# Gated attention and channel mixer on one core: the first turn's scores made in the strip schedule, its operands fetched and rounded on other engines, and the score banks paired by when they come free

## The chip, the core and the metric

The kernel runs on one core of a Trainium2 chip. The metric is the device time of one execution in microseconds (us). Three runs of the kernel before took 1034.19 to 1035.68 us, with a median of 1035.26 us.

## What is computed

Two branches work on the same 2048 tokens of 448 numbers, and a gate mixes them for each token:

```python
g = sigmoid((x * gate_w).sum(-1))
qkv = x @ wqkv                                  # 16 heads of 28
p = softmax(q @ k.T * 28 ** -0.5)               # per head, 2048 x 2048
a = (p @ v) @ wo
b = gelu(layernorm(x) @ w1 + b1) @ w2 + b2      # 448 -> 1792 -> 448
out = g * a + (1 - g) * b
```

## The kernel before

**Strips.** The first part of the program makes q, k and v, then the mixer branch. Every product there is cut into four strips of 32 rows of the TensorE array (partitions 0 to 31, 32 to 63 and so on), which run at the same time. Numbers are held as a rounded high part and the rest as a low part, so a product takes three passes: high by high, high by low, low by high. A planner in the kernel (`Strips.run`) walks through the four strips with a clock of its own, costs and due times, and writes out the order of the instructions once: for each free strip it takes a piece that is under way or opens the next tile in one of the six PSUM banks 0 to 5 (`pick`), and it calls DMAs and roundings when their due time has come (`run_tasks`). The mixer's second product (`Down`, line 503 as all strip work) is evicted by ScalarE (line 410) and stored to `gbs` by a DMA on ScalarE's queue (line 413).

**Row maxima.** Between these pieces stand single matmuls of queries by keys (`RowMax.one`, line 212), each followed by a maximum on VectorE (line 214). They give the shift of the softmax, 1024 of them in all. Some 570 are done within the strips, the rest later.

**Turns.** Attention is a loop of turns, written out by `turn_of` and `batch`. A unit is one head by one block of 128 keys by 512 queries; a turn scores four units (line 1168) and multiplies the four of the turn before by v (line 1212, `batch`). The scores of a unit are three matmuls into one PSUM bank (`score`), each on one strip. A turn has two banks called `first`, two called `second` and two called `spare`; these come from `pairs`, which is turned by one place from turn to turn, so that the six banks 0 to 5 go round in three turns. The order within a turn is: a row maximum into bank 6; the two `first` units alone (step 0); both pairs (steps 1 and 2); then `soften` of the first pair, one exponential on ScalarE over both banks (line 1174); the last pass of the second pair (step 3); `soften` of the second pair, one exponential per bank as long as row maxima are left; a row maximum into the first spare bank; and the products by v in bank 7. `pairs` before holds the first banks 0, 2 and 4, so that a pair is always two neighbouring banks, and the exponential of a pair reads 1024 consecutive words per partition.

**Between strips and turns** stand four matmuls of `idle` (line 974) that compute nothing that is used, and six more after the first turn's scores. The first turn is scored like every other; its keys and queries come by GpSimd's queue (lines 848 and 865), and GpSimd rounds them (lines 853, 854, 869, 870) when the last `Up` piece is done (`early`). Twelve tiles of the output are projected (`project`) in turns near the end, four in the last lines.

Of the kernel before, what the change touches and what calls it, by code (L numbers as in the profile page):

```python
# [7 lines left out]
F32 = mybir.dt.float32  # L8
# [27 lines left out]
def kernel(ctx: ExitStack, tc: tile.TileContext, xt, wqk, wv, wo, xk, w1, b1, w2, b2,  # L36
# [336 lines left out]
    class Down(Piece):  # L373
# [31 lines left out]
        def close(self, st, now):  # L405
            if self.i > 1:
                gb = mhp[0].tile([P, CH], F32, name="h", bufs=2)[:, :D]
            else:
                gb = mhp[0].tile([P, D], F32, name="gb", bufs=2)
            nc.scalar.activation(gb, bk[:, self.bank, :D], AF.Copy)  # L410
            st.use("act", now + 0.2, 0.56)
            st.free[self.bank] = st.act + 0.1
            nc.scalar.dma_start(gbs[self.c * TPC + self.i], gb)
            st.use("act", now, 0.5)

    class Strips:


        def __init__(self, tiles):
            self.tiles = tiles  # L420
            self.t = [0.0] * 4
            self.visit, self.held = [None] * 4, [None] * 4
            self.feed, self.stat = Feed(self, []), Feed(self, bxr)
            self.live = []
            self.free = {b: 0.0 for b in range(6)}
            self.rm = {6: 0.0, 7: 0.0}
            self.dve = self.act = self.pool = -1.0
            self.clock = self.dma = -1.0
# [6 lines left out]
            self.handed = 0  # L435

        def use(self, engine, start, cost):
            setattr(self, engine, max(getattr(self, engine), start) + cost)
# [20 lines left out]
                    self.use(engine, t, cost)  # L459

        def pick(self, s, now, over=None):
            for x in self.live:
                if x.bar(self):
                    continue
                if x.next(s) and not x.busy and x.ready <= now and (over is None or isinstance(x, Up) and x.c == over.c):
                    return x
            if over is None and self.tiles and self.tiles[0].next(s) and self.tiles[0].start(self, now):
                b = min(self.free, key=lambda b: self.free[b], default=None)
                if b is not None and self.free[b] <= now:
                    x = self.tiles.pop(0)  # L470
                    x.bank = b
                    x.begin(s)
                    del self.free[b]
                    self.live.append(x)
                    started(self, x, now)
                    return x
            return None

        def run(self):
            while self.tiles or self.live:  # L480
# [22 lines left out]
                mm = nc.tensor.matmul(bk[:, x.bank, :n], a, b, start=x.first, stop=(len(x.rem) == 1 and m == len(ops) - 1),  # L503
                                      skip_group_check=True)
# [377 lines left out]
    def early(st, now):  # L882

        m0.close()
        st.at(now + 2.0, lambda: nc.scalar.activation(gate, zall, AF.Exp, scale=-1.0), act=1.6)
        st.at(now + 6.0, gates, dve=0.7)
        ak = ctx.enter_context(tc.tile_pool(name="ak", bufs=1, side="right", reuse_waits="tile"))
        ka, kb, la, lb = (ak.tile([P, S], F32R, name=n) for n in ("ka", "kb", "la", "lb"))
        va, vb = (ak.tile([P, NT, P], F32, name=n) for n in ("va", "vb"))
        for d, a, b in ((khi, ka, kb), (klo, la, lb), (vg, va, vb)):  # L890
            d.update({0: a, 1: b, 2: a, 3: b})
        st.at(now + 4.0, lambda: nc.gpsimd.memset(la.bitcast(F32), 0.0), pool=2.2)
# [5 lines left out]
        st.at(now + 10.0, lambda: load_v(0, slice(0, 8)))  # L898
        st.at(now + 11.5, lambda: load_v(0, slice(8, 16)))
        st.at(now + 16.0, lambda: load_ms(0))  # L900
        st.at(now + 23.0, lambda: key_row(0))
        st.at(now + 23.5, lambda: nc.gpsimd.memset(lb.bitcast(F32), 0.0), pool=2.2)

    for v in vt:
        nc.gpsimd.memset(v[:, :, DH:DH + 1], 1.0)
# [61 lines left out]
    m1.close()  # L967
    loads[0] = nc.sync

    pairs = sorted((0, 2, 4), key=lambda b: max(strips.free[b], strips.free[b + 1]))  # L970

    def idle(n, b):
        for _ in range(n):
            nc.tensor.matmul(bk[:, b], khi[0][:, 0:P], khi[0][:, 0:CH], start=True, stop=True)  # L974

    idle(4, min(range(6), key=lambda b: strips.free[b]))

    def sb(name, bufs):
        return ctx.enter_context(tc.tile_pool(name=name, bufs=bufs, reuse_waits="tile"))
# [159 lines left out]
                tail.append((turn + (12 if c == 1 else 8) + i, c * TPC + i))  # L1139

    UNITS = NG * NC * 64
    prob, tail = {}, []
    begins = set()
    projected = set()
    cold = [1] * 4
# [24 lines left out]
    def soften(u, half, b, count, step=4):  # L1170
        t = ap.tile([P, 2, CH], F32, name=f"p{half}")
        for i in range(0, count, step):
            e = min(i + step, count)
            nc.scalar.activation(t[:, i:e], bk[:, b + i:b + e], AF.Exp, scale=SCALE)  # L1174
        for i in range(count):
            prob[u + i] = t[:, i]

    def turn_of(u, turn):

        left = UNITS - u  # L1180
        size = min(left, 4)
        for x in range(u, u + size):
            n = x // 64
            if n not in begins:
                begins.add(n)
                begun(n, turn)
# [3 lines left out]
        ahead = [(u + i) % 4 for i in range(2)]  # L1190
        behind = [(u + i) % 4 for i in range(2, 4)]
        if rowmax.left() and turn not in projected:
            lone(behind, 6, turn)
        for step in range(4):
            for i in range(na):
                if step < 3:
                    score(u + i, step, first + i)
            for i in range(nb):
                if step > 0:
                    score(u + 2 + i, step - 1, second + i)  # L1200
            if step == 2:
                soften(u, 0, first, na)
        if nb:
            soften(u + 2, 1, second, nb, 1 if rowmax.left() else 2)
        if rowmax.left():
            lone(ahead, spare, turn)
        return size

    def batch(b, turn):
# [83 lines left out]
```

## Time and profile before

| | |
|---|---|
| median of three runs | 1035.26 us |
| the profiled execution's own time | 1034.85 us |
| its span, from the first to the last instruction | 1033.1 us |
| TensorE busy | 1024.8 us (99%) |
| VectorE busy | 749.2 us (73%) |
| ScalarE busy | 662.9 us (64%) |
| GpSimd busy | 372.9 us (36%) |
| mean granted TensorE clock | 0.998 |

One execution was taken by the hardware profiler. PE is TensorE's matmuls, PEld its weight loads, ACT is ScalarE, DVE VectorE, POOL GpSimd and SP the engine that issues most DMAs; a q behind a name is that engine's DMA queue. Times count from the first instruction. A timeline row has the start, the length, the engine and the line, the operation with its tiles, and how many instructions were merged into it; in brackets stands how long the engine had stood idle and which engine released it. A group's row has the time that its instructions took together and the mean of one in ns. A row of a table by stretch has the stretch, its length and then the busy time of PE, PEld, DVE, ACT and POOL with the number of instructions, the granted clock, the DMA engines' share and their rate.

### The profile page before, as it was taken

How to read it: one execution, taken by the hardware profiler on the slowest of the kernel's cores; microseconds unless marked ns; L12 is line 12 of the kernel's file. 1: busy time of each engine (PE TensorE's matmuls, PEld its weight loads, DVE VectorE, ACT ScalarE, POOL GpSimd, SP SyncE). 2: the span in 40 equal slices, each digit the busy share in tenths (PEclk: the TensorE clock that was granted, in tenths of full speed). 3: DMA queues.
4: the chain of work that ended last, by engine and by line, in shares of the span. 5: the costliest groups of instructions: out<-in, count | busy, mean ns of one | idle time of the engine just before them, and what ended most of it. 6: DMA issues, size and time to landing. Idle time of an engine off the chain costs nothing.

```text
span 1033.1 us, 30973 instructions
## 1 busy us (share of the span) xinstructions
PE 1024.8 (99%) x13170; PEld 676.9 (66%) x13170; DVE 749.2 (73%) x1178; ACT 662.9 (64%) x1018; POOL 372.9 (36%) x396
## 2 busy tenths in 40 slices
PE   9999999999999999999999999999999999999997
PEld 6999999999999999944444444444444444454555
DVE  4899999999999999956666666656666666644101
ACT  5234365034043043089999999999999999959553
POOL 5467569626334036460011001410111223626414
PEclk9999999999999999999999999999999999999999
DMA  7697533221110013251000010310002201121202
GB/s 242 201 264 250 181 109 101 83 65 45 39 38 11 9 42 87 67 145 29 14 18 26 21 36 15 102 34 24 17 27 59 56 12 58 21 73 31 73 29 81
DMA packets 47787, 73.20 MB, mean 71 GB/s; under 512 B 13840, under 2 KB 28816, under 8 KB 46848
## 3 DMA queue, kind: packets, MB, share of 16 engines
q1 hardware_dynamic: 33888, 39.11, 13.5%
q0 software_dynamic: 5120, 16.89, 5.7%
q10 hardware_dynamic: 8640, 15.21, 4.1%
q8 instruction: 103, 1.69, 0.7%
q14 instruction: 36, 0.29, 0.1%
HBM read 51.75 MB, written 19.31 MB: 69 GB/s over the span
## 4 chain that ended last, share of the span: by engine, by line
PE 98%; DMA 1%; DVE 0%; ACT 0%; SPq 0%; issue 0%; ACTq 0%; DVEq 0%
PE bk L503 36%; PE bk L1212 25%; PE bk L1168 17%; PE bk L212 16%; PE bk L1030 2%; PE bk L1032 1%; PE bk L1031 1%; PE bk L949 1%; DMA first<-in_xt 1%; DVE raw L715 0%; PE bk L974 0%; DVE mx L214 0%; ACT gb L410 0%; PE bk L1095 0%; SPq L927 0%
## 5 line engine op out<-in xcount | busy, mean ns | idle before, releaser
L214 DVE TENSOR_REDUCE mx<-bk 128x1 f32<-128x512 f32 x1024 | 683.7, 689 | 179.6 <-PE bk L212 155.0
L1174 ACT ACTIVATE p<-bk 128x1024 f32<-128x1024 f32 x745 | 510.9, 758 | 63.7 <-PE bk L1168 37.7
L212 PE MATMUL bk<-kd,qd 28*128 28x512 f32 x1024 | 436.1, 427 | 0.7 <-DVE mx L214 0.6
L212 PEld LDWEIGHTS bk<-kd,qd 28*128 28x128 f32 x1024 | 186.1, 182 | 199.5 <-DVE mx L214 176.7
L503 PE MATMUL bk<-yh,w1f 32*128 32x512 f32 x1568 | 186.4, 391 | 0.0
L503 PE MATMUL bk<-yl,w1f 32*128 32x512 f32 x784 | 161.8, 390 | 0.0
L503 PEld LDWEIGHTS bk<-yh,w1f 32*128 32x128 f32 x1568 | 151.1, 183 | 0.7 <-ACT gb L410 0.2
L503 PE MATMUL bk<-w2h,hh 32*128 32x448 f32 x896 | 143.7, 365 | 0.0
L503 PE MATMUL bk<-w2l,hh 32*128 32x448 f32 x896 | 142.5, 363 | 0.0
L1070 POOL TENSOR_TENSOR ot<-ob,rc 128x512 f32<-128x512 f32 x12 | 15.4, 1286 | 348.0 <-DMA rc<-rls 289.4
L1212 PE MATMUL bk<-p,vb 128*32 128x512 f32 x1024 | 136.6, 605 | 0.0
L1212 PE MATMUL bk<-p,va 128*32 128x512 f32 x1024 | 136.4, 605 | 0.0
L367 POOL TENSOR_TENSOR hl<-h,hh 128x512 fp32r<-128x512 f32 x56 | 72.6, 1308 | 124.4 <-PE bk L503 48.3
L503 PEld LDWEIGHTS bk<-yl,w1f 32*128 32x128 f32 x784 | 104.0, 183 | 0.0
L503 PEld LDWEIGHTS bk<-w2h,hh 32*128 32x128 f32 x896 | 103.4, 183 | 0.3
L503 PEld LDWEIGHTS bk<-w2l,hh 32*128 32x128 f32 x896 | 102.9, 183 | 0.1
L1168 PE MATMUL bk<-yh,ka 29*128 29x512 f32 x512 | 93.2, 470 | 0.1
L503 PE MATMUL bk<-w2h,hl 32*128 32x448 f32 x896 | 88.8, 362 | 0.0
L1168 PE MATMUL bk<-yh,kb 29*128 29x512 f32 x512 | 88.1, 477 | 0.0
L359 ACT ACTIVATE h<-bk,b1s 128x512 f32<-128x512 f32 x56 | 38.3, 683 | 67.9 <-PE bk L503 56.9
L1168 PE MATMUL bk<-yh,la 28*128 28x512 f32 x512 | 80.3, 393 | 0.0
L1168 PE MATMUL bk<-yl,ka 28*128 28x512 f32 x512 | 79.7, 390 | 0.0
(141 smaller groups left out, 1554.1 us busy)
## 6 DMA issues: line engine op xcount, KB each, us to landing
qk<-qo ACTq DMA_DIRECT2D x28, 256.0 KB
raw<-in_xt SPq DMA_DIRECT2D x17, 256.0 KB
vs<-vt ACTq DMA_DIRECT2D x16, 256.0 KB
rc<-rls SPq DMA_DIRECT2D x60, 64.0 KB
bxr<-in_xk POOLq DMA_DIRECT2D x8, 448.0 KB, 6.0
acc<-gbs SPq DMA_DIRECT2D x16, 224.0 KB
out_y<-acc SPq DMA_DIRECT2D x16, 224.0 KB
qd<-qk SPq DMA_DIRECT2D x60, 56.0 KB
```

The lines of the kernel that those rows point to most:

```text
L212: nc.tensor.matmul(ps, self.qd[n % 2][r, i * P:(i + 1) * P], self.kd[r, k * 512:(k + 1) * 512], start=True, stop=True)
L214: nc.vector.reduce_max(self.mx[n % 2][:, j, i, k:k + 1], ps, axis=AX)
L359: nc.scalar.activation(h, bk[:, self.bank], AF.Gelu_apprx_tanh, bias=b1s[:, f:f + 1])
L367: nc.gpsimd.tensor_sub(hl[f], h, hh[f].bitcast(F32))
L503: mm = nc.tensor.matmul(bk[:, x.bank, :n], a, b, start=x.first, stop=(len(x.rem) == 1 and m == len(ops) - 1), skip_group_check=True)
L949: nc.tensor.matmul(bk[:, b], w, v, start=(i == 0), stop=(i == len(ops) - 1), skip_group_check=True)
L1030: nc.tensor.matmul(po, h, woh[:, g], start=(g == 0), stop=False, skip_group_check=True)
L1031: nc.tensor.matmul(po, h, wol[:, g], start=False, stop=False, skip_group_check=True)
L1070: nc.gpsimd.tensor_mul(ot[g][:, c * CH:(c + 1) * CH], ob, rc)
L1168: nc.tensor.matmul(bk[:, b], w[r, ks], q[r], start=(p == 0), stop=(p == 2), skip_group_check=True)
L1174: nc.scalar.activation(t[:, i:e], bk[:, b + i:b + e], AF.Exp, scale=SCALE)
L1212: nc.tensor.matmul(bk[32 * j:32 * j + 32, 7], vg[n // NC][:, k, 32 * j:32 * j + 32], prob[4 * b + j], start=(k == 0), stop=(k == NT - 1), ...
```

## The change

It has seven parts. A new piece `Unit` scores one of the first four units within the strip schedule: three matmuls on one strip, an exponential into the space of `vg[1]`, open to the planner once no tile is left to open and 16 us of the planner's clock have gone by since the last `Up` piece. The loop of turns then starts at unit 4, so that turn 0 scores units 4 to 7 and multiplies units 0 to 3 by v. The keys and queries of the first units are fetched by SyncE with earlier due times, the high parts are made by ScalarE, the low parts by GpSimd, and the row of ones goes into the unrounded keys. The last four mixer tiles are stored by SyncE. The ten `idle` matmuls are gone. `pairs` is no longer (0,1), (2,3), (4,5): the six banks are sorted by the time at which the planner has them free, and taken two by two, so a pair can be two banks that are not neighbours; `soften` reads them with a step between the banks. In turns after a projection the two halves of the units may change places.

```diff
+    SCORED = 16.0
...
             nc.scalar.activation(gb, bk[:, self.bank, :D], AF.Copy)
...
+            if self.c == NC - 1:
+                nc.sync.dma_start(gbs[self.c * TPC + self.i], gb)
+                return
             nc.scalar.dma_start(gbs[self.c * TPC + self.i], gb)
...
+    class Unit(Piece):
+        cost = 0.235
...
+        def start(self, st, now):
+            return st.scored <= now
+
+        def ops(self, s):
+            r, top = slice(32 * s, 32 * s + DH), slice(32 * s, 32 * s + DH + 1)
+            h, l, q, ql_ = khi[0], klo[0], qh[0], ql[0]
+            return [(h[top, 0:P], q[top]), (l[r, 0:P], q[r]), (h[r, 0:P], ql_[r])]
+
+        def close(self, st, now):
+            t = vg[1][:, 4 * self.i:4 * self.i + 4].rearrange("p t d -> p (t d)")
+            nc.scalar.activation(t, bk[:, self.bank], AF.Exp, scale=SCALE)
+            prob[self.i] = t
...
         def pick(self, s, now, over=None):
+            if over is None and not self.tiles:
+                x = next((x for x in self.units if x.next(s) and x.start(self, now)), None)
...
-        st.at(now + 4.0, lambda: nc.gpsimd.memset(la.bitcast(F32), 0.0), pool=2.2)
+        loads[0] = nc.sync
+        st.scored = now + SCORED
+        st.at(now + 0.3, lambda: nc.gpsimd.memset(la.bitcast(F32), 0.0), pool=1.9)
         for j in range(4):
-            st.at(now + 3.5 + 1.5 * j, lambda j=j: fetch_qq(0, j))
-            st.at(now + 6.5 + 1.5 * j, lambda j=j: fetch_kk(0, j))
-            st.at(now + 14.5 + 2.0 * j, lambda j=j: split_kk(0, j), pool=1.9)
-        st.at(now + 12.0, lambda: split_qq(0), pool=1.9)
...
+            st.at(now + 0.6 + 0.6 * j, lambda j=j: fetch_qq(0, j))
+            st.at(now + 3.5 + 0.6 * j, lambda j=j: fetch_kk(0, j))
+        st.at(now + 3.2, lambda: loads[0].dma_start(la[DH:P:32].bitcast(F32), ones))
+
+        def high(h, l):
+            nc.scalar.activation(h, l.bitcast(F32), AF.Copy)
...
+                nc.gpsimd.tensor_sub(l, l.bitcast(F32), h.bitcast(F32))
...
-    pairs = sorted((0, 2, 4), key=lambda b: max(strips.free[b], strips.free[b + 1]))
-
-    def idle(n, b):
-        for _ in range(n):
-            nc.tensor.matmul(bk[:, b], khi[0][:, 0:P], khi[0][:, 0:CH], start=True, stop=True)
-
-    idle(4, min(range(6), key=lambda b: strips.free[b]))
+    order = sorted(range(6), key=lambda b: strips.free[b])
+    pairs = [sorted(order[i:i + 2]) for i in (0, 2, 4)]
...
-            nc.scalar.activation(t[:, i:e], bk[:, b + i:b + e], AF.Exp, scale=SCALE)
+            nc.scalar.activation(t[:, i:e], bk[:, b[i]:b[e - 1] + 1:b[1] - b[0]], AF.Exp, scale=SCALE)
...
+        if turn in projected and size == 4 and sum(rowmax.cnt[s] for s in behind) < sum(rowmax.cnt[s] for s in ahead):
+            ahead, behind, order = behind, ahead, [2, 3, 0, 1]
...
-    u = b = turn = 0
+    u, b, turn = 4, 0, 0
+    begins.add(0)
+    begun(0, 0)
...
-        if turn == 0:
-            idle(6, 7)
```

**From the strips to the turns, on TensorE.** The program before has, behind the last strip matmul (`w2h`, `hl`), the dummies, the twelve score matmuls of turn 0 (keys `ka` and `la`, queries `yh` and `yl`), more dummies and the first row maximum (`kd`, `qd`) of turn 1:

```order
L503 MATMUL bk<-w2h_3803,hl_2961 128x448 x2
L974 MATMUL bk<-ka 128x512 x4
L1168 MATMUL bk<-yh,ka 128x512 x2
L1168 MATMUL bk<-yh,la 128x512 x2
L1168 MATMUL bk<-yh,ka 128x512 x2
L1168 MATMUL bk<-yl,ka 128x512 x2
L1168 MATMUL bk<-yh,la 128x512 x2
L1168 MATMUL bk<-yl,ka 128x512 x2
L974 MATMUL bk<-ka 128x512 x6
L212 MATMUL bk<-kd,qd_153 128x512
```

The changed program, at the same place; `vb` holds the exponentials of units 0 to 3:

```order
L543 MATMUL bk<-w2h_3803,hl_2961 128x448
L1218 MATMUL bk<-yh,ka 128x512 x2
L1218 MATMUL bk<-yh,la 128x512 x2
L1218 MATMUL bk<-yh,ka 128x512 x2
L1218 MATMUL bk<-yl,ka 128x512 x2
L1218 MATMUL bk<-yh,la 128x512 x2
L1218 MATMUL bk<-yl,ka 128x512 x2
L1264 MATMUL bk<-vb,va 32x512 x4
L212 MATMUL bk<-kd,qd_153 128x512
```

The dummies are gone, turn 0 has products by v, and the twelve score matmuls of units 0 to 3 have moved up among the strip matmuls, in two groups of six, the first with 142 rows of strip work behind it, the second with 188. One row maximum more stands in the strips (570 for 569), and there are 255 turns with scores instead of 256.

**Within a turn, on TensorE, with the counters that a row waits for.** `Activation_49` counts ScalarE's instructions, `DVE_49` VectorE's. This is turn 2 of the program before, from the `first` scores to the products by v:

```order
L1168 MATMUL bk<-yh,ka 128x512 [waits DVE_49]
L1168 MATMUL bk<-yh,ka 128x512
L1168 MATMUL bk<-yh,la 128x512 x2
L1168 MATMUL bk<-yh,ka 128x512 [waits Activation_49]
L1168 MATMUL bk<-yh,ka 128x512
L1168 MATMUL bk<-yl,ka 128x512 x2
L1168 MATMUL bk<-yh,la 128x512 x2
L1168 MATMUL bk<-yl,ka 128x512 x2
L212 MATMUL bk<-kd,qd_152 128x512 [waits Activation_49]
L1212 MATMUL bk<-p_9804,va 32x512 x2
L1212 MATMUL bk<-p_9808,va 32x512
L1212 MATMUL bk<-p_9808,va 32x512 [waits Activation_49]
```

Its three waits for ScalarE are for exponentials of the turn before, by the counts that the program holds. In the changed program these rows reach from the last score row of turn 3 to the last but one of turn 4:

```order
L1218 MATMUL bk<-yl,ka 128x512 [waits Activation_49]
L212 MATMUL bk<-kd,qd_153 128x512
L1264 MATMUL bk<-p_9845,va 32x512 x2
L1264 MATMUL bk<-p_9849,va 32x512 x2
L212 MATMUL bk<-kd,qd_153 128x512 [waits DVE_49]
L1218 MATMUL bk<-yh,ka 128x512 [waits DVE_49]
L1218 MATMUL bk<-yh,ka 128x512
L1218 MATMUL bk<-yh,la 128x512 x2
L1218 MATMUL bk<-yh,ka 128x512 x2
L1218 MATMUL bk<-yl,ka 128x512 x2
L1218 MATMUL bk<-yh,la 128x512 x2
L1218 MATMUL bk<-yl,ka 128x512 [waits Activation_49]
```

The last pass of the `second` pair (`yl`, `ka` at the end of a turn) now waits for ScalarE, in turn 3 its second matmul, in turn 4 its first, and the count is that of the first exponential of the same turn. In turn 5 it is the row maximum behind the scores that does so:

```order
L1218 MATMUL bk<-yh,la 128x512 x2
L1218 MATMUL bk<-yh,ka 128x512 x2
L1218 MATMUL bk<-yl,ka 128x512 x2
L1218 MATMUL bk<-yh,la 128x512 x2
L1218 MATMUL bk<-yl,ka 128x512 x2
L212 MATMUL bk<-kd,qd_153 128x512 [waits Activation_49]
```

The pairs that the planner's times give are the banks 2 and 5, 1 and 3, 0 and 4. In turns whose number divides by three the exponential of the first pair reads banks 2 and 5, and the row that waits for it writes bank 3; in the next turn it reads 0 and 4, and bank 2 waits; in the third it reads 1 and 3, and the row maximum into bank 2 waits. Of the 255 turns with scores 247 have such a wait for the first exponential of their own turn; the other 8 are turns of the third kind after the last row maximum. In those last turns the exponential of the second pair is one instruction over two banks as well, and the next turn's first matmul into a bank between them waits for it.

More of the change, by code (lines that the diff above doesn't have):

```diff
@@ L435, in __init__ @@
             self.handed = 0
+            self.units, self.scored = [Unit(j) for j in range(4)], 1e9
         def use(self, engine, start, cost):
@@ L461, in pick @@
         def pick(self, s, now, over=None):
+            if over is None and not self.tiles:
+                x = next((x for x in self.units if x.next(s) and x.start(self, now)), None)
+                b = min(self.free, key=lambda b: self.free[b], default=None)
+                if x is not None and b is not None and self.free[b] <= now:
+                    self.units.remove(x)
+                    x.bank = b
+                    del self.free[b]
+                    self.live.append(x)
+                    return x
             for x in self.live:
@@ L479, in run @@
         def run(self):
-            while self.tiles or self.live:
+            while self.tiles or self.live or self.units:
                 s = min(range(4), key=lambda s: (self.t[s], s))
@@ L891, in early, with low @@
             d.update({0: a, 1: b, 2: a, 3: b})
-        st.at(now + 4.0, lambda: nc.gpsimd.memset(la.bitcast(F32), 0.0), pool=2.2)
+        loads[0] = nc.sync
+        st.scored = now + SCORED
+        st.at(now + 0.3, lambda: nc.gpsimd.memset(la.bitcast(F32), 0.0), pool=1.9)
         for j in range(4):
-            st.at(now + 3.5 + 1.5 * j, lambda j=j: fetch_qq(0, j))
-            st.at(now + 6.5 + 1.5 * j, lambda j=j: fetch_kk(0, j))
-            st.at(now + 14.5 + 2.0 * j, lambda j=j: split_kk(0, j), pool=1.9)
-        st.at(now + 12.0, lambda: split_qq(0), pool=1.9)
[L898 to L902, printed above, removed]
+            st.at(now + 0.6 + 0.6 * j, lambda j=j: fetch_qq(0, j))
[3 more added lines that the diff above has]
+            nc.scalar.activation(h, l.bitcast(F32), AF.Copy)
+            st.use("act", st.clock, 0.65)
+            def low():
+                nc.gpsimd.tensor_sub(l, l.bitcast(F32), h.bitcast(F32))
+                st.use("pool", st.clock, 1.35)
+            st.at(st.act + 0.1, low)
+        st.at(now + 7.0, lambda: high(qh[0], ql[0]))
+        for i in range(4):
+            sl = slice(i * CH, (i + 1) * CH)
+            st.at(now + 10.5 + 1.4 * i, lambda sl=sl: high(ka[:, sl], la[:, sl]))
+        st.at(now + 10.6, lambda: load_ms(0))
+        st.at(now + 11.5, lambda: load_v(0, slice(0, 8)))
+        st.at(now + 13.0, lambda: load_v(0, slice(8, 16)))
+        st.at(now + 19.0, lambda: nc.gpsimd.memset(lb.bitcast(F32), 0.0), pool=2.2)
     for v in vt:
@@ L1141 @@
     UNITS = NG * NC * 64
-    prob, tail = {}, []
+    tail = []
     begins = set()
@@ L1189, in turn_of @@
         nb = size - na
-        ahead = [(u + i) % 4 for i in range(2)]
-        behind = [(u + i) % 4 for i in range(2, 4)]
+        ahead, behind = ([(u + i) % 4 for i in x] for x in ((0, 1), (2, 3)))
+        order = list(range(size))
+        if turn in projected and size == 4 and sum(rowmax.cnt[s] for s in behind) < sum(rowmax.cnt[s] for s in ahead):
+            ahead, behind, order = behind, ahead, [2, 3, 0, 1]
         if rowmax.left() and turn not in projected:
@@ L1196, in turn_of @@
                 if step < 3:
-                    score(u + i, step, first + i)
+                    score(u + order[i], step, first[i])
             for i in range(nb):
                 if step > 0:
-                    score(u + 2 + i, step - 1, second + i)
+                    score(u + order[2 + i], step - 1, second[i])
             if step == 2:
-                soften(u, 0, first, na)
+                soften(u + order[0], 0, first, na)
         if nb:
-            soften(u + 2, 1, second, nb, 1 if rowmax.left() else 2)
+            soften(u + order[2], 1, second, nb, 1 if rowmax.left() else 2)
         if rowmax.left():
-            lone(ahead, spare, turn)
+            lone(ahead, spare[0], turn)
         return size
```

6 lines of the change are left out of this document (added).

## Prediction

> **What bounds the kernel now.** First the page's busy times and its chain of waits.
>
> ```profile
> PE 1024.8 (99%) x13170; PEld 676.9 (66%) x13170; DVE 749.2 (73%) x1178; ACT 662.9 (64%) x1018; POOL 372.9 (36%) x396
> ...
> PE bk L503 36%; PE bk L1212 25%; PE bk L1168 17%; PE bk L212 16%; PE bk L1030 2%; PE bk L1032 1%; PE bk L1031 1%; PE bk L949 1%; DMA first<-in_xt 1%; DVE raw L715 0%; PE bk L974 0%; DVE mx L214 0%; ACT gb L410 0%; PE bk L1095 0%; SPq L927 0%
> ```
>
> TensorE is busy 99% of the span, and 98% of the chain is its rows: any time in which it has to stand still is added to the end, and what other engines do in that time is not. So I read next the timeline of TensorE over one turn, the loop that runs 255 times, and ScalarE's row in the same turn.
>
> ```profile
> 446.88 0.50 PE L212 MATMUL bk<-kd,qd 28*128 28x512 f32 x1
> 446.88 0.73 PE L1168 MATMUL bk<-yh,ka 29*128 29x512 f32 x4
> 447.22 0.41 PE L1168 MATMUL bk<-yh,la 28*128 28x512 f32 x3
> 447.46 0.39 PE L1168 MATMUL bk<-yl,ka 28*128 28x512 f32 x2
> ...
> 447.69 0.38 PE L212 MATMUL bk<-kd,qd 28*128 28x512 f32 x1
> 448.01 1.07 PE L1212 MATMUL bk<-p,va 128*32 128x512 f32 x8
> 449.01 0.49 PE L212 MATMUL bk<-kd,qd 28*128 28x512 f32 x1
> ```
>
> ```profile
> 447.96 1.02 ACT L1174 ACTIVATE p<-bk 128x1024 f32<-128x1024 f32 x1 [0.19 <-PE bk L1168]
> ```
>
> The turn starts at 446.88 and the next at 449.01: 2.13 us. The first pair's last pass (`yl`, `ka`) starts at 447.46 and ends at 447.85; the exponential of that pair runs from 447.96 to 448.98. The second pair's last pass and the row maximum beside it start at 447.69, the products by v at 448.01. What matters: in this kernel the second pair's last pass is long over when the first pair's exponential ends. Over 500 us the lengths are the same every time:
>
> ```profile
> L1174 ACT ACTIVATE p<-bk 128x512 f32<-128x512 f32 x459 | 248.7, 600 | 0.0
> L1174 ACT ACTIVATE p<-bk 128x1024 f32<-128x1024 f32 x230 | 235.4, 1023 | 40.6 <-PE bk L1168 15.2 <-PE bk L212 0.8
> ```
>
> Last the place between strips and turns, TensorE and ScalarE.
>
> ```profile
> 438.22 1.19 PE L974 MATMUL bk<-ka 128*128 128x512 f32 x4
> ...
> 440.14 0.49 PE L1168 MATMUL bk<-yh,ka 29*128 29x512 f32 x1
> ...
> 440.49 0.39 PE L1168 MATMUL bk<-yl,ka 28*128 28x512 f32 x1
> ...
> 441.04 1.66 PE L974 MATMUL bk<-ka 128*128 128x512 f32 x6
> 442.63 0.49 PE L212 MATMUL bk<-kd,qd 28*128 28x512 f32 x1
> ```
>
> ```profile
> 439.55 0.54 ACT L410 ACTIVATE gb<-bk 128x448 f32<-128x448 f32 x1 [0.46 <-ACT gb L410]
> 440.12 0.33 ACTq L413 DMA_DIRECT2D gbs<-gb  x1
> 440.55 0.55 ACT L410 ACTIVATE h<-bk 128x448 f32<-128x448 f32 x1 [0.46 <-PE bk L1168]
> ```
>
> From 438.22, the first dummy, to 442.63, the first row of turn 1, go 4.41 us, for twelve score matmuls that elsewhere take under one.
>
> **The sum's base** is the profiled execution's own time, 1034.85 us, of which the span is 1033.1 and 1.75 lies around it. It is 0.41 below the median of the runs shown, which is no difference here.
>
> **The passage from strips to turns.** The 4.41 us go: dummies, the wait for evictions, the scores of turn 0. In their place the strips get 13 more matmuls, twelve scores and a row maximum. The strips' pace is read from a stretch of the same work:
>
> ```profile
> 400.00:420.00 20.00, 20.00 (x361) 19.80 (x358) 19.47 (x35) 3.97 (x6) 13.62 (x18) 1.00 0.57 135
> ```
>
> 20 us by 361 is 0.055 us, by 13 is 0.72. The number of full turns doesn't change: before, turn 0 lay in the 4.41 us and 255 turns with scores and products followed; now there are 255 in all. So this part saves 4.41 - 0.72 = 3.7 us. If the 13 go into gaps of the strips it is 4.2; if their data are late, less, and that is the next part.
>
> **Operands of the first units.** They are needed earlier: the first `Unit` row stands behind 24 row maxima after the last `Up` matmul, at these two rows' distance.
>
> ```profile
> 401.56 0.39 PE L503 MATMUL bk<-yl,w1f 32*128 32x512 f32 x1
> ...
> 416.99 0.50 PE L212 MATMUL bk<-kd,qd 28*128 28x512 f32 x1
> ```
>
> ```profile
> 405.32 1.83 POOL L892 MEMSET la<- 128x2048 f32 x1
> ...
> 410.99 0.51 POOL L848 DMA_DIRECT2D la<-qk  x1
> ...
> 418.76 0.61 POOL L853 CAST ka<-la 128x512 fp32r<-128x512 f32 x1 [2.45 <-DMA la<-qk]
> 419.45 1.30 POOL L854 TENSOR_TENSOR la<-la,ka 128x512 fp32r<-128x512 f32 x1
> ```
>
> The clearing of `la` moves to about 402.6, ahead of GpSimd's last low part, and SyncE, which has no loads of v in between, can issue the keys by about 407. The slowest case of before, 7.3 us from the end of the last issue (411.5) to the rounding (418.76), gives 414.3; 0.6 for the high part on ScalarE, idle then, and 1.3 for the low part give 416.2, before 417. I cost this at nothing. The cover is 0.8 us; without it TensorE, which takes its rows in order, stands still for what is missing, 1 us or so. The low part of the last `Up` piece comes 1.8 us later, behind the clearing; the planner counts that and puts other strip rows first. The stores on SyncE wait for ScalarE's evictions, the last of which ends at 440.55 + 0.55 = 441.1 now, and behind them are queued `wo` and the next units' queries: those begin later by some us, but are read only when turns have begun that use them. On ScalarE four issues of 0.33 go away, 1.3 us together, so the evictions end near 439.8 and the first exponential of turn 0 isn't kept from starting. Also nothing. This part with the last: 2.5 to 4.2 us saved, 3.7 taken, as both rows of the strips' pace and of the loads say so.
>
> **The turn.** Here the change costs. The pairs are banks 2 and 5, 1 and 3, 0 and 4, and the rows of the built program show what comes of it: in 247 of 255 turns a matmul into a bank that lies between the two waits for the exponential of the same turn's first pair, though that exponential doesn't read it. TensorE takes its rows in order, so the row maximum and the products by v are queued behind it. From the turn above: the exponential ends at 447.96 + 1.02 = 448.98. An eviction's end at 439.55 + 0.54 = 440.09 let a matmul start at 440.14, so 0.05 more: 449.03. Without the wait the row started at 447.69. That is 1.34. A matmul after a standstill is followed by the next on its strip after 0.35 (440.14 to 440.49), in a running turn after 0.24 (447.22 to 447.46), which adds 0.11. So a turn is longer by 1.45 us and takes 3.58. Nothing hides it: the exponential cannot start before the first pair's last pass, which TensorE itself does at a fixed place of the turn. ScalarE needs at most 1.02 + 2 x 0.60 = 2.2 us per turn, so it doesn't become the bound.
>
> Bounds for one turn: 1.29 if there is neither hop nor restart (448.98 - 447.69); 1.63 if a whole weight load of 0.18 comes on top, the mean of these loads:
>
> ```profile
> L212 PEld LDWEIGHTS bk<-kd,qd 28*128 28x128 f32 x371 | 67.5, 182 | 153.9 <-DVE mx L214 145.0 <-DVE lt L1059 5.9 <-DVE mf L229 1.7
> ```
>
> 247 x 1.45 = 358 us (319 to 403). The other 8 turns make the next one wait for the exponential of the second pair, which ends 1.08 + 2 x 1.02 = 3.1 us after the turn's start where the next started after 2.1; 1 us each, partly behind projections: 5 us (0 to 9).
>
> The Trainium skill, PSUM — Partial Sum Buffer, section "PSUM bank collisions raise a hardware error", says that accesses are to be guarded by bank and quadrant, and that engines in different banks don't disturb each other. By that rule a matmul into bank 3 needs no wait for a reader of 2 and 5, and the sum would be the saving alone, 1031.2. The wait is in the program all the same.
>
> **Sum:** 1034.85 - 3.7 + 358 + 5 = 1394 us; from the bounds 1034.85 - 4.2 + 319 = 1350 to 1034.85 - 2.5 + 403 + 9 = 1444.
>
> **Rivals.** *The clock falls too.* TensorE will pause in every turn, from about 448.09 (or 447.87) to 449.03, so it is busy 68 to 74% of a turn of 3.58. The table by stretch shows what pauses did before:
>
> ```profile
> 1026.42:1029.83 3.41, 1.44 (x8) 0.97 (x6) 2.16 (x4) 0.00 (x0) 0.00 (x0) 1.00 0.65 239
> 115.05:118.47 3.42, 2.80 (x53) 2.78 (x57) 3.42 (x6) 0.63 (x1) 3.36 (x4) 1.00 0.49 150
> ```
>
> ```profile
> 1028.00:1031.00 3.00, 0.00 (x0) 0.00 (x0) 0.58 (x1) 0.00 (x0) 0.00 (x0) 0.80 0.71 258
> ```
>
> After a stretch with 42% busy the clock was halved within it or just behind (0.80 in 1028 to 1031); a stretch with 82% kept it. 70% is nearer to the latter. If the clock is halved throughout, TensorE's own 2.13 us of each turn double at most: 255 x 2.13 = 543 more, 1937; if half the time, 1666. The Trainium skill, TensorE: Matmul & The Clock Gate, Part 1, says that the clock falls after about 3.4 us without work; by that rule it stays up here, where pauses are 1.2 at most. The row of 1028 disagrees in part, since the last matmul ended less than 2 us before the fall.
>
> *Not slower.* If the row's wait is already met when TensorE comes to it, only the saving is left: 1031.2. That needs the exponential to end by 447.69 of such a turn, 1.29 us earlier than now, or a program on the chip without these waits. The timeline speaks against the first, the rows against the second.
>
> *Only two kinds of turns are long.* In the third kind just a row maximum waits; if the 77 such turns cost nothing, 1394 - 77 x 1.45 = 1282. Against it: the products stand behind it in order.
>
> **Chances.** About 0.2% is what a measurement of this kernel can tell from no change. The forecast with its bounds has 0.81: its mechanism is in the rows, and its terms are measured lengths. The clock has 0.12, two kinds only 0.03, not slower 0.04 (0.03 faster by over 0.2%, 0.01 within). The range is that of the forecast alone, 1350 to 1444; it leaves out 0.19. Faster 0.03, same 0.01, slower 0.96.
>
> **What would show it.** In the changed kernel's timeline a turn should take 3.58 us, with TensorE idle about 1 us in each, ended by ScalarE's exponential (line 1224) ahead of the scores (line 1218) in two turns of three and of the row maximum (line 212) in the third; turns start near 439, and the clock stays at 1.00. TensorE busy falls from 99% to about 75%. Turns of 2.13 us would make it all wrong; turns of 3.5 with a clock under 0.9 the second case; a third of the turns at 2.13 the fourth. A stop ahead of a `Unit` row near 417 would show the operands late.

## The result and the profile after

The changed kernel took 1417.76 us (median of four runs, 1411.43 to 1443.13) against 1034.72 before: a ratio of 1.368, 95% interval 1.363 to 1.373. Ratios here and below leave out runs that are some per cent longer at a lower mean clock: the one of 1443.13 here (0.955), and one of the ten with one exponential per bank (1102.65, 0.851). The forecast was 1394, its range 1350 to 1444. A second set, taken with the experiments, gave 1419.87 (six runs, 1414.12 to 1433.51), ratio 1.374 (1.368 to 1.379). The profiled run of the first set is the one of 1443.13, so the rows here are those of the same kernel profiled again, an execution of 1414.12 us.

The page's busy times and its chain of waits:

```profile
PE 1131.3 (80%) x13160; PEld 696.7 (49%) x13160; DVE 749.5 (53%) x1178; ACT 684.5 (48%) x1024; POOL 363.1 (26%) x379
...
PE 78%; ACT 18%; issue 2%; DMA 0%; DVE 0%; ACTq 0%; SPq 0%; DVEq 0%
```

TensorE has gone from 99% to 80% of the span (about 75% was forecast), and ScalarE, which had 0% of the chain, holds 18% of it. TensorE's busy time itself rose from 1024.8 us although it has ten matmuls fewer: its rows are longer at half clock, and also behind a stop, as 0.49 against 0.40 below. What TensorE waits for, in total, times and longest, from the table of waits:

```profile
PE bk L1218 <- ACT p L1224: 198.6, 175, 1.5
PE bk L212 <- ACT p L1224: 74.3, 77, 1.2
```

These are 252 waits for an exponential, 77 of them by the row maximum (line 212); the forecast had 255 (247 and 8), 77 of them there. Two turns on TensorE, the next one's first row, and ScalarE beside the second of them:

```profile
499.58 0.50 PE L212 MATMUL bk<-kd,qd 28*128 28x512 f32 x1
...
501.73 0.50 PE L212 MATMUL bk<-kd,qd 28*128 28x512 f32 x1 [0.95 <-ACT p L1224]
502.16 1.06 PE L1264 MATMUL bk<-p,va 128*32 128x512 f32 x8
503.16 0.50 PE L212 MATMUL bk<-kd,qd 28*128 28x512 f32 x1
503.16 0.51 PE L1218 MATMUL bk<-yh,ka 29*128 29x512 f32 x3
...
503.74 0.40 PE L1218 MATMUL bk<-yl,ka 28*128 28x512 f32 x2
505.32 0.49 PE L1218 MATMUL bk<-yl,ka 28*128 28x512 f32 x1 [1.18 <-ACT p L1224]
505.33 0.49 PE L212 MATMUL bk<-kd,qd 28*128 28x512 f32 x1
505.75 1.07 PE L1264 MATMUL bk<-p,va 128*32 128x512 f32 x8
506.74 0.49 PE L212 MATMUL bk<-kd,qd 28*128 28x512 f32 x1
```

```profile
504.25 2.20 ACT L1224 ACTIVATE p<-bk 128x1024 f32<-128x1024 f32 x3 [1.59 <-PE bk L1218]
```

From 499.58 to 503.16 and from 503.16 to 506.74 is 3.58 us, the forecast's length to the hundredth. In the first, a turn of the third kind, the row maximum is held back until 501.73. In the second the last pass of the second pair is held back until 505.32, just behind the end of the exponential that begins at 504.25 and takes 1.02, and the row maximum and the products come after it. The three instructions that are merged on ScalarE end at 506.45, and it then stands idle till the next turn's first pair: each of the two engines now waits for the other.

What the forecast had at 1.00 throughout is the clock. A table by stretch, each 3.41 us long (length, busy times of PE, PEld, DVE, ACT and POOL, then the granted clock):

```profile
1337.12:1340.53 3.41, 2.23 (x19) 0.87 (x19) 0.00 (x0) 2.05 (x2) 0.00 (x0) 1.00 0.00 0
1340.53:1343.95 3.42, 2.23 (x23) 0.88 (x22) 0.00 (x0) 2.05 (x2) 0.00 (x0) 1.00 0.03 5
1343.95:1347.36 3.41, 3.21 (x23) 0.83 (x19) 0.00 (x0) 1.94 (x2) 0.00 (x0) 0.50 0.01 2
...
1357.59:1361.01 3.42, 3.42 (x13) 2.85 (x10) 0.00 (x0) 0.00 (x0) 0.00 (x0) 0.50 0.00 0
1361.01:1364.42 3.41, 3.41 (x28) 1.81 (x27) 0.68 (x1) 1.44 (x2) 0.00 (x0) 1.00 0.18 67
```

The first two stretches are both 65% busy (a pause of 1.18 us in 3.41): after the one the clock stayed, after the other it was halved at 1343.95. It came back at 1361.01, behind a stretch in which TensorE was busy without a gap.

### The profile page after: what moved, and what is told of

Read it like the earlier page. It is cut to its first block, busy times and chain, and to the rows that moved or that the text cites. A ratio compares the mean times of both kernels' runs of the same rounds, so it can differ in the third digit from the quotient of the medians.

```text
span 1441.0 us, 31026 instructions
## 1 busy us (share of the span) xinstructions
PE 1162.5 (81%) x13160; PEld 705.0 (49%) x13160; DVE 749.0 (52%) x1178; ACT 684.7 (48%) x1024; POOL 362.5 (25%) x379
## 4 chain that ended last, share of the span: by engine, by line
PE 78%; ACT 18%; issue 2%; DMA 0%; DVE 0%; POOL 0%; ACTq 0%; SPq 0%; DVEq 0%
PE bk L543 25%; PE bk L1264 19%; ACT p L1224 18%; PE bk L1218 17%; PE bk L212 13%; PE bk L1080 1%; PE bk L1082 1%; PE bk L1081 1%; PE bk L1004 1%; DMA first<-in_xt 0%; DVE raw L755 0%; ACTq L1224 0%; POOL yl L777 0%; POOL raw L760 0%; ACT yh L776 0%
## 5 line engine op out<-in xcount | busy, mean ns | idle before, releaser
L1224 ACT ACTIVATE p<-bk 128x1024 f32<-128x1024 f32 x742 | 527.4, 756 | 458.3 <-PE bk L1218 415.1
L212 PE MATMUL bk<-kd,qd 28*128 28x512 f32 x1024 | 470.7, 460 | 73.5 <-ACT p L1224 72.9
L1218 PE MATMUL bk<-yl,ka 28*128 28x512 f32 x508 | 113.0, 440 | 96.5 <-ACT p L1224 96.5
L1218 PE MATMUL bk<-yl,kb 28*128 28x512 f32 x512 | 110.9, 441 | 96.9 <-ACT p L1224 96.9
L1264 PE MATMUL bk<-p,vb 128*32 128x512 f32 x1024 | 147.4, 649 | 0.0
L1264 PE MATMUL bk<-p,va 128*32 128x512 f32 x1016 | 145.6, 647 | 0.0
L1218 PEld LDWEIGHTS bk<-yl,ka 28*128 28x128 f32 x508 | 55.4, 197 | 139.2 <-ACT p L1224 136.0
L1218 PEld LDWEIGHTS bk<-yl,kb 28*128 28x128 f32 x512 | 53.9, 198 | 139.9 <-ACT p L1224 135.9
L1218 PE MATMUL bk<-yh,ka 29*128 29x512 f32 x508 | 98.6, 498 | 0.0
L1218 PE MATMUL bk<-yh,kb 29*128 29x512 f32 x512 | 92.9, 507 | 5.3 <-ACT p L1224 5.3
```

What stands on the lines that cost most here:

```text
L212: nc.tensor.matmul(ps, self.qd[n % 2][r, i * P:(i + 1) * P], self.kd[r, k * 512:(k + 1) * 512], start=True, stop=True)
L1218: nc.tensor.matmul(bk[:, b], w[r, ks], q[r], start=(p == 0), stop=(p == 2), skip_group_check=True)
L1224: nc.scalar.activation(t[:, i:e], bk[:, b[i]:b[e - 1] + 1:b[1] - b[0]], AF.Exp, scale=SCALE)
L1264: nc.tensor.matmul(bk[32 * j:32 * j + 32, 7], vg[n // NC][:, k, 32 * j:32 * j + 32], prob[4 * b + j], start=(k == 0), stop=(k == NT - 1), ...
```

## The experiments

Each experiment shows its edit, then what was expected, then the result. The theory is that the program holds back a matmul into any bank that lies between the two banks that an exponential reads, and that this is the whole loss, with the clock adding to it where the pauses let it fall. The rivals are: another of the seven parts costs the time; banks that are not neighbours cost it on the chip itself; the wait is made up later.

**Neighbouring banks.** The changed kernel with one line put back.

```diff
-    order = sorted(range(6), key=lambda b: strips.free[b])
-    pairs = [sorted(order[i:i + 2]) for i in (0, 2, 4)]
+    pairs = [[b, b + 1] for b in sorted((0, 2, 4), key=lambda b: max(strips.free[b], strips.free[b + 1]))]
```

> The changed kernel with pairs of neighbouring banks again, (2,3), (0,1), (4,5); all other parts of the change stay. Theory (the program holds back a matmul into a bank that lies between the two that the first pair's exponential reads): no turn waits for an exponential of its own turn, turns of 2.13 us, clock at 1.00 as before, and the passage from strips to turns 3.7 us shorter: 1031 us (1029 to 1034). Rival A (the loss comes from another part: no dummy matmuls, so a low clock at the start of the turns, or the operands): still over 1300. Rival B (the pairs cost something but the clock falls without the dummies): one stretch of half clock of some 30 us near 440, in which turns of 2.13 take 4.2, 15 us more, 1046.

1030.26 us (1028.80 to 1032.27), ratio 0.996 (0.993 to 0.999); clock 1.00. A turn of it on TensorE:

```profile
499.91 0.49 PE L212 MATMUL bk<-kd,qd 28*128 28x512 f32 x1
499.92 0.73 PE L1217 MATMUL bk<-yh,ka 29*128 29x512 f32 x4
...
501.05 1.06 PE L1263 MATMUL bk<-p,va 128*32 128x512 f32 x8
502.04 0.49 PE L212 MATMUL bk<-kd,qd 28*128 28x512 f32 x1
```

The turn is 2.13 us long, with no stop. The other six parts together cost nothing and gain a little; rivals A and B are out.

**The kernel before with the banks apart**, and nothing else of the change.

```diff
-    pairs = sorted((0, 2, 4), key=lambda b: max(strips.free[b], strips.free[b + 1]))
+    pairs = [[2, 5], [1, 3], [0, 4]]
...
-            nc.scalar.activation(t[:, i:e], bk[:, b + i:b + e], AF.Exp, scale=SCALE)
+            nc.scalar.activation(t[:, i:e], bk[:, b[i]:b[e - 1] + 1:b[1] - b[0]], AF.Exp, scale=SCALE)
```

> The kernel before with nothing changed but the pairs, (2,5), (1,3), (0,4), and the exponential's step between banks. Theory: the same long turns, 3.58 us instead of 2.13 in all but a few of 256, and the clock falls now and then as in the changed kernel: 3.7 us above the changed kernel, 1415 to 1422, 1398 if the clock held. Rival A (the loss needs the other parts): 1035.

1418.92 us (1417.55 to 1421.97), ratio 1.373 (1.371 to 1.375), clock 0.980 to 0.985. Its waits:

```profile
PE bk L1168 <- ACT p L1174: 198.5, 175, 1.7
PE bk L212 <- ACT p L1174: 74.3, 77, 1.2
```

They are as many as in the changed kernel, and within 0.1 us as long in all. The pairs alone make the whole loss, in either kernel.

**One exponential for each bank**, pairs as in the changed kernel.

```diff
-                soften(u + order[0], 0, first, na)
+                soften(u + order[0], 0, first, na, 1)
...
-            soften(u + order[2], 1, second, nb, 1 if rowmax.left() else 2)
+            soften(u + order[2], 1, second, nb, 1)
```

> The changed kernel with the same pairs of banks that aren't neighbours, but each exponential reads one bank, so that none spans another's bank. Theory: the wait for the same turn's exponential is gone; ScalarE has four exponentials of one bank per turn, 4 x 0.545 = 2.18 us by the two that follow one another in 1.09, which is a little over TensorE's 2.13, so ScalarE sets the turn: 2.18 to 2.26 us, 1031 + 231 x 0.05 to 0.13 = 1043 to 1061 us. Rival (it is the place of the banks on the chip that hurts, not the span of the read): over 1300.

1031.56 us in the median, nine of the ten runs within 1030.35 and 1031.69, ratio 0.997 (0.996 to 0.998). TensorE waits for no exponential any more. The rival is out: the same six banks, in the same places, cost nothing when no single read spans another pair's bank. The price that I had put on it, 12 to 30 us, did not come. These are ScalarE's rows over 5.83 us:

```profile
499.60 5.83 ACT L1224 ACTIVATE p<-bk 128x512 f32<-128x512 f32 x11
```

Eleven in 5.83 us is 0.53 each where they follow without a gap, so four take 2.12, just under TensorE's 2.13 for a turn. My 0.545 came from two in a row, whose last one I counted in full.

**One pair that spans the others.**

```diff
-    pairs = [sorted(order[i:i + 2]) for i in (0, 2, 4)]
+    pairs = [[1, 2], [3, 4], [0, 5]]
```

> The changed kernel with the pairs (1,2), (3,4), (0,5): only one of the three pairs spans other banks, so one turn of three, 85 in all, has a row that waits for the same turn's exponential. Theory: those turns 3.58 us, the others 2.13: 1031 + 85 x 1.45 = 1154 us (1140 to 1165 for the bounds 1.29 and 1.63 with what the clock does); a stretch of 3.4 us is on the mean busier than in the changed kernel, so the clock falls more seldom or not at all. Rival (any pair with a step costs the same, whatever lies between): over 1300; rival (the wait of one turn is caught up in the next two): 1031 to 1060.

1163.76 us (1162.74 to 1166.33), ratio 1.126 (1.124 to 1.128), clock 0.995 to 0.998. Three turns on TensorE:

```profile
499.99 0.49 PE L212 MATMUL bk<-kd,qd 28*128 28x512 f32 x1
...
502.12 0.50 PE L212 MATMUL bk<-kd,qd 28*128 28x512 f32 x1
...
504.25 0.49 PE L212 MATMUL bk<-kd,qd 28*128 28x512 f32 x1
...
506.41 0.50 PE L1217 MATMUL bk<-yl,ka 28*128 28x512 f32 x2 [1.19 <-ACT p L1223]
...
507.84 0.49 PE L212 MATMUL bk<-kd,qd 28*128 28x512 f32 x1
```

They take 2.13, 2.13 and 3.59 us: one turn of three is long, by the amount that was worked out, and nothing is made up in the next two. The 10 us above 1154 lie mostly in the last 24 turns, where the second pair's exponential reads both banks too and, when these are 0 and 5, the next turn waits for it (3.1 us where the kernel before has 1.9 to 2.2, six times).

**The clock, first try.** Three matmuls whose result isn't used, where TensorE waits, in the turns that have row maxima.

```diff
+            if step == 2 and size == 4 and turn < 232:
+                for _ in range(3):
+                    nc.tensor.matmul(bk[:, 6], khi[u // 64 // NC][:, 0:P], qh[u // 64 % 3], start=True, stop=True)
             if step == 2:
```

> The changed kernel, its pairs as they are, with three matmuls that compute nothing that is used (into the row maximum's bank 6) behind the second step of each turn up to 231, where TensorE would stand still for the exponential. Theory of the wait: the turn stays 3.58 us, since these rows lie within the wait. Theory that the clock is the rest of the miss (1417 where 1394 was forecast, and runs from 1411 to 1443): TensorE is now busy some 90% of a turn, the clock stays up to turn 231, and the time is 1394 to 1402 with runs close to each other; the changed kernel has 1417. Rival (the clock has nothing to do with the pauses, or the extra is longer turns): 1411 to 1418 again, at a clock of 0.98. Rival (the three rows delay what waits): over 1420.

1418.68 us (1411.85 to 1423.35): no gain, so by the total the theory missed. The trace, of a run of 1423.35, shows two things. Up to 1297 us the clock stood at 1.00, but the three rows made the turns a little longer: 818.5 us for the first 223, where the repeated run of the changed kernel below takes 814.8, ten microseconds of these at half clock. After that, in the last 24 turns, where nothing was filled, it fell five times for 10.24 us each. That left open whether the pauses are what the clock goes by.

**The clock, second try**: two rows in turns up to 231, three later, and four behind the second exponential of those late turns whose next one waits for it; the changed kernel ran beside it.

```diff
+            if step == 2 and size == 4:
+                for _ in range(3 if turn > 231 else 2):
+                    nc.tensor.matmul(bk[:, 6], khi[u // 64 // NC][:, 0:P], qh[u // 64 % 3], start=True, stop=True)
             if step == 2:
...
         if rowmax.left():
             lone(ahead, spare[0], turn)
+        elif turn % 3 == 2 and size == 4:
+            for _ in range(4):
+                nc.tensor.matmul(bk[:, 6], khi[u // 64 // NC][:, 0:P], qh[u // 64 % 3], start=True, stop=True)
```

> The changed kernel, its pairs as they are, with unused matmuls in every place where TensorE stands still in a turn: two behind the second step in turns up to 231, three after that, and four behind the second exponential in turns of the third kind without row maxima. In the run with three of them up to turn 231 the clock stayed at 1.00 that long, but the turn was 3.62 instead of 3.59 us and the clock fell five times after turn 231. Theory (what the changed kernel takes above the forecast is the clock): clock at 0.998 or more, turns of 3.59, and 1030.3 + 223 x 1.457 + 8 x 1.46 + 31 for the last 24 turns = 1398 (1394 to 1404), all runs within some 4 us; the changed kernel beside it 1411 to 1420 and at a clock under 0.99. Rival (the rows fill the gaps, but the pauses are not what the clock goes by): clock of 0.98 and 1415.

> The changed kernel again, beside the one with the filled gaps: 1411 to 1420 us with a clock of 0.98 to 0.99 in most runs. By the theory its time above 1398 is a third of the time that it spends at half clock (a turn at half clock takes 5.4 us instead of 3.59).

Filled: 1412.91 us, all five runs within 1412.62 and 1413.38, clock 0.999 to 1.000. Unfilled: 1419.87, from 1414.12 to 1433.51, clock 0.965 to 0.984. A late stretch of the filled one:

```profile
1300.00:1400.00 100.00, 98.25 (x591) 52.37 (x590) 6.74 (x12) 39.75 (x42) 26.50 (x23) 1.00 0.12 38
```

TensorE is busy 98% there, the clock doesn't fall, and the runs differ by 0.8 us instead of 19. So in this kernel the clock falls because of the pauses, and the spread between its runs is the clock's. The time itself is 15 us over the expected 1398, since the rows did not only fill gaps: from the products of turn 231 to those of turn 255 it takes 113.7 us, where the unfilled one would take 100 at full clock, summed over its own turns that were not slowed (2.15, 3.59 and 4.74 without a projection, 4.55 and 6.22 with one). Turns of 2.15 became 4.59.

**Where the small gain comes from.** First the kernel before with the stores of the last four tiles on SyncE and without dummies, then without dummies alone (the diff is that of the first; the second lacks its top part, the store).

```diff
-            nc.scalar.dma_start(gbs[self.c * TPC + self.i], gb)
+            (nc.sync if self.c == NC - 1 else nc.scalar).dma_start(gbs[self.c * TPC + self.i], gb)
...
-    idle(4, min(range(6), key=lambda b: strips.free[b]))
...
-        if turn == 0:
-            idle(6, 7)
```

> The kernel before with two of the seven parts: the last four mixer tiles stored by SyncE, and no dummy matmuls; turn 0 is scored like every other. It asks where the gain of 4 us of the kernel with neighbouring banks (1030.3) comes from. Theory A (the passage was long by the dummies and by the DMA issues between the evictions): the four evictions follow one another in 2.1 us and end 1.3 us earlier, the last six dummies (1.66 us) are gone, turn 1 starts near 439.8 instead of 442.6: 2.9 us saved, 1031.4. Theory B (it takes the scoring within the strips): 1034 or little less. Rival C (without the dummies the clock falls near 440): 10 us or more slower.

> The kernel before without the ten dummy matmuls, nothing else. Theory A: the first four lie beside the wait for the evictions and cost nothing, the last six cost their 1.66 us: 1032.6, unless the clock falls. Rival C (they keep the clock up): in the stretch of 3.4 us around 440 TensorE is then busy less than 65%, the clock falls for one or more such stretches, and the time is 1036 or more.

Both parts: 1032.88 us (1031.34 to 1035.11), ratio 0.9985 (0.9976 to 0.9994). Dummies alone: 1036.62 (1035.66 to 1037.68), ratio 1.0021 (1.0012 to 1.0030). With both, ScalarE and TensorE:

```profile
440.02 0.54 ACT L410 ACTIVATE h<-bk 128x448 f32<-128x448 f32 x1 [32.60 <-PE bk L503]
440.46 0.97 ACT L410 ACTIVATE gb<-bk 128x448 f32<-128x448 f32 x2
441.31 0.56 ACT L410 ACTIVATE h<-bk 128x448 f32<-128x448 f32 x1
```

```profile
443.17 0.50 PE L1167 MATMUL bk<-yh,ka 29*128 29x512 f32 x2 [0.51 <-ACT p L1173]
```

The evictions follow one another as said, in 1.85 us, but turn 1 then stops 0.51 for turn 0's exponential, which theory A had left out. By the medians 1.8 us are gained, a little over half of what theory A said, so neither theory holds as it stands. The figure is not a close one: in the profiled run, of 1034.95 us, the clock was also halved once from 8.83 to 12.25, far ahead of the parts in question, and the six of the eleven runs at a mean clock of 0.999 or more took 1031.34 to 1032.88. Without the dummies alone the evictions still wait for their issues, TensorE pauses twice in the first stretch below (0.43 and 0.27), and the clock falls:

```profile
438.19:441.60 3.41, 2.68 (x18) 1.16 (x17) 0.89 (x3) 1.85 (x4) 1.34 (x2) 1.00 0.68 218
441.60:445.01 3.41, 3.06 (x17) 1.29 (x19) 0.96 (x2) 3.25 (x5) 2.00 (x3) 0.50 0.77 237
```

So the dummies of the kernel before did earn their time there, as rival C has it. With the scores in the strips, the stores off ScalarE and neighbouring banks they have nothing left to fill: that kernel's trace has no pause of TensorE in this passage.

**Neighbouring banks again**, the best version, beside the two.

> The changed kernel with neighbouring banks once more, with five rounds, for a narrower interval beside the two partial versions: 1030.3 us, 4.0 less than before, ratio 0.996.

1030.29 us (1029.99 to 1031.74), ratio 0.996 (0.995 to 0.997). That is faster than both kernels, and by 4.4 us than the one before.

## Why the prediction was right, step by step

**The wait.** Right in mechanism, place and size. 1.45 us per turn was forecast; the turn is 3.58 to 3.59 against 2.13. The Trainium skill, PSUM — Partial Sum Buffer, section "PSUM bank collisions raise a hardware error", has engines in different banks not disturb each other. The run with one exponential per bank (1031.56) agrees, for the chip: TensorE waits for no exponential there, whichever bank is being read. It is the program that makes it wait.

**The eight other turns.** Forecast 1 us each, 5 together since some are hidden behind projections. They are found where the next turn begins, in the repeated profile of the changed kernel; 252 less 247 leaves five such waits:

```profile
1292.75 0.51 PE L1218 MATMUL bk<-yh,kb 29*128 29x512 f32 x4 [1.08 <-ACT p L1224]
...
1294.91 0.49 PE L1218 MATMUL bk<-yl,kb 28*128 28x512 f32 x1 [1.19 <-ACT p L1224]
```

TensorE idles 1.08 and restarts, and the turn's own wait of 1.19 follows. Four of the five are 1.08 to 1.11 us long, the fifth, at half clock, 0.20.

**The passage.** 3.7 us saved was forecast. From the last `Up` matmul to the first products by v it was 401.56 (shown above) to 443.76 before, 42.20 us, and is 38.64 with neighbouring banks:

```profile
443.76 0.64 PE L1212 MATMUL bk<-p,va 128*32 128x512 f32 x4
```

```profile
400.54 0.39 PE L543 MATMUL bk<-yl,w1f 32*128 32x512 f32 x1
...
439.18 0.64 PE L1263 MATMUL bk<-vb,va 128*32 128x512 f32 x4
```

So 3.56 us are saved. Their cause is not a single part: stores and dummies without the scores in the strips gave 2.2 of it in the profile. In the changed kernel itself the passage is shorter by 2.6 only, since the first long turn's wait of 1.0 lies in it, and in the run at a clock of 0.955 the clock was halved at its end, from 440.12 to 470.84.

**The operands.** Forecast at nothing with a cover of 0.8 us. The cover is larger: with neighbouring banks the first low part ends at 411.99 + 5.05 / 4 = 413.3 and its reader starts at 417.2, 3.9 us later. In the changed kernel too no matmul waits for a low part.

```profile
411.99 5.05 POOL L945 TENSOR_TENSOR la<-la,ka 128x512 fp32r<-128x512 f32 x4 [6.11 <-ACT ka L941]
...
417.21 0.39 PE L543 MATMUL bk<-yh,la 28*128 28x512 f32 x1
```

**Not forecast: the end.** From the start of the last matmul to the end of the span it takes 1033.1 - 1027.49 = 5.6 us before and 1027.5 - 1022.94 = 4.6 with neighbouring banks. The rows of the last matmul:

```profile
1027.49 0.37 PE L1032 MATMUL bk<-woh,ol 128*128 128x448 f32 x1
```

```profile
1022.94 0.37 PE L1081 MATMUL bk<-woh,ol 128*128 128x448 f32 x1
```

The last stores are issued at the same distance from it in both; the microsecond is gone from what stands behind them. The kernels built on the one before all have the longer end, those built on the changed one the shorter (4.7 against 5.2 us behind the last matmul's end in the kernel with the nested pairs, 4.2 in the others). Which part does it was not tried.

**The clock: the step that was mis-sized.** The prediction said of a stretch about 70% busy that it "is nearer to the latter", the 82% that kept the clock, and so the forecast held it at 1.00 and the rival halved it throughout or half the time. It was neither. The turns have stretches of 65%; of these most keep the clock and a few don't. Each fall lasts until a stretch that is busy throughout (twice 92 and 98%), and a turn at half clock takes 5.4 us instead of 3.59. The ten runs of the changed kernel lie on a line. With the time at half clock as twice what the mean clock lacks of 1, times the run's length, 40 us of it (clock 0.986) go with 1411.4, 45 (0.984) with 1414.1, 100 (0.965) with 1433.5 and 130 (0.955) with 1443.1: 1398 us plus 0.35 for each us at half clock. By this line the kernel would take an estimated 1398 at full clock, which none of its runs had: 4 over the forecast of 1394. The other 20 of the median are the clock. That the median lies within the stated range all the same is in part luck: the range's upper end was made for longer waits, which didn't come, and the clock used up that room, in one run to within 1 us of the end. The rival had the right mechanism and the wrong price, because it knew only two cases.

**The rivals.** "Not slower" fell with the first row of waits; "two kinds only" with the 77 waits of the row maximum, whose turns (499.58 to 503.16 above) are as long as the others.

## What to carry to other kernels

A read with a step over a shared buffer can count, for whatever orders the program, as a read of everything in between: before spreading the buffers of a pair, list for one whole round of the loop which instruction each engine waits for, and look for a wait for an instruction of the same turn where there were only waits for the turn before. A wait of this kind has a price that can be read from one turn of the old trace, end of the reader minus the start of the row that is held back, and it is paid in every turn. And pauses of a third of the time may or may not take the clock: give that case its own, partial price, and look at how much of the array works in the rest of the time.

## What the runs showed of the hardware

In all profiled runs the granted clock changes only at steps of 3.41 us. Of 28 rises after the first 13 us of a program, 26 followed a stretch of that length in which TensorE was busy without a gap, and the other two one of 98% and 92%. Of 31 falls after that (not counting those behind an empty stretch at the very end), 29 came behind a stretch that was 16 to 65% busy, and two others at 72 and 78%, both at the passage; but of the stretches at 64 to 66%, about 300 kept the clock and 11 did not. The Trainium skill, TensorE: Matmul & The Clock Gate, Part 1, has in its table of states the clock fall after an idle window of about 3.4 us and rise after a busy one: the step and the rise agree, the fall does not, since the longest wait in the table of waits of the run shown above is 1.6 us.

Busy time counts a single strip like all four. The same traces separate the falls better when each matmul's length is weighted with the part of the array that it occupies (a quarter for a matmul on one strip of 32 rows or on 32 columns, all for 128x128), added up over the stretch and divided by 3.41 us; overlapping matmuls can take it above 1. Below 0.65, 24 stretches lost the clock and none kept it; from 0.65 to 0.70, 4 lost it and 25 kept it; above 0.70, 3 lost it and some 4000 kept it. The two stretches of 65% shown above have 0.67, which kept it, and 0.62, which lost it. This was found afterwards, and no run has tested it.

Pauses in every turn aren't the only way to a lower clock: one run with one exponential per bank had a mean of 0.851, and one of the kernel before 0.948 (1041.84 us). Neither was profiled, and their cause is open.

ScalarE's exponential over one bank costs 0.53 us where another follows at once and 0.60 alone; over two banks it takes 1.02, neighbours or not.
